# Queue order, pool opening and adding transfers in a one-core FNet and mixture-of-experts kernel

## The chip, the core and the metric

The kernel runs on one core of one Trainium2 chip. A core has a matrix engine (PE, with weight loads counted apart as PEld), three engines for element-wise work (DVE, the vector engine; ACT, the scalar engine; POOL, GpSimd) and SP, which here only issues transfers. Each engine takes its instructions from a queue of its own, in order; an instruction that waits holds up everything behind it on that engine. Transfers are issued on three queues: SP's (q1 in the profile), ACT's (q10) and POOL's (q0). The metric is the device time of one execution in microseconds (us).

## What is computed

A block of 2048 tokens with 512 features is normalised. Two things are computed from the result and added to the input: a two-dimensional Fourier mixing (two dense products with cosine and sine matrices) and a mixture of 8 experts in which every token goes to one.

```python
xn = layernorm(x)                                   # 2048 x 512
a, b = xn @ dft_hid_re.T, xn @ dft_hid_im.T         # over the features
y = dft_seq_re @ a - dft_seq_im @ b                 # over the tokens, 2048 x 2048 each
logits = xn @ w_gate                                # 512 x 8
e = first_argmax(logits)                            # one expert per token, its gate softmax over one value
out = x + y + gate * (silu(xn @ w1[e]) @ w2[e])     # w1: 512 x 1376, w2: 1376 x 512
```

## The kernel before

Every product is done with numbers split into a high and a low part (`hi` and `lo`): three matmuls, hi by hi, lo by hi and hi by lo, stand for one product. `split` (line 68) makes the parts: ACT copies `raw` to `hi`, DVE subtracts to get `lo`. `stream` (line 76) loads a 512 KB block on SP's queue into one of three `raw` slots (`RAWS`) and splits it into one of four `hi` and `lo` slots. All blocks stand in one list; `need(key, ahead)` (line 90) brings the list up to a key and some blocks further, so it sets what is written when. A transfer's issue waits until its slot is free.

In order of time, PE does this:

- **Head and first products** (to about 102 us). `two_products(0, ...)` multiplies token blocks b = 0 to 7 by the cosine blocks `c(0, 0, b)` and the sine blocks `c(0, 1, b)` of the first quarter of the outputs. Each b first needs the normalised block: `Norm` loads x, takes statistics on DVE, a root on ACT, factors on DVE, then ACT writes `xh` and `xn`, and DVE writes `xl`. The norm of b = 0 is done in two halves (`n0`, `n1`) in an order fixed by hand for DVE and ACT, together with the split of the first blocks (lines 213 to 233). The norms of later blocks are placed by `pre0(b)`. The tile framework's scheduler orders the rest on each engine, from priorities and a model of times.
- **Second quarter** (to 192 us), with the gate's logits on DVE beside it (`logits`, line 339; the gate's weights lie in `wgb`, copied to all partitions); then `count`, `route` and `scatter`, which sorts the tokens by expert into `xs` in memory.
- **`even_product(0)` and `(1)`** (to 283 us): products with sums of blocks. Their results are stored by ACT's queue to `p2`, `q6`, `v`, `c00` and `r`; `sum_up(ri)` (line 480) then adds stored blocks in memory, by three transfers on POOL's queue that add to their target.
- **Experts** (to about 579 us): 8 windows of sorted tokens, each with eleven steps `f`: `up` (weights w1), SiLU on ACT (`sil`), its split on DVE (`hh`, `hl`), and, two steps later, `down` (weights w2). Weight blocks come in the list as `w(i, k, b)`: window, matrix, block. Every fifth block of the list takes its slots from an extra pool, `more` (line 100), once that is open. It is opened at line 764, right after `head.close()`, whose place in memory it takes: its first transfer must wait until the head's last tile is released.
- **`odd_product(0)` and `(1)`** (to 648 us) and **`second_product(0 to 3)`** (to the end), with `fetch_product` loading the stored intermediate products (`pd` and others) for the last product.

At several places a line asks for its written order, `tc.keep_in_program_order`; SP's transfers have no such order in general.

Of the kernel before, what the change touches and what calls it, by code (L numbers as in the profile page):

```python
# [44 lines left out]
def fnet_moe(ctx, tc, x, cr, ci, dr, di, wg, w1, w1r, w2, w2r, out):  # L45
# [141 lines left out]
    for i in range(WARM):  # L187
# [7 lines left out]

    n0, n1 = Norm(0, 0, 1), Norm(0, 1, 1)
    first = [tuple(st.tile([P, 1024], F32 if n == "raw" else F32R, tag=n, name=n, bufs=RAWS if n == "raw" else 4)
                   for n in ("raw", "hi", "lo")) for ri in range(2)]
    halves = [slice(j * TC, (j + 1) * TC) for j in range(2)]
    for j, n in enumerate((n0, n1)):  # L200
        n.load()
        for ri in range(2):
            SY.dma_start(first[ri][0][:, halves[j]], (cr, ci)[ri][0, 0, :, j, :])

    def first_hi(ri, j):
        raw, hi, _ = (t[:, halves[j]] for t in first[ri])
        A.copy(hi, raw)

    def first_lo(ri, j):
        raw, hi, lo = (t[:, halves[j]] for t in first[ri])  # L210
        V.tensor_sub(lo, raw, hi.bitcast(F32))
# [22 lines left out]
    for ri in range(2):  # L234
        ready["c", 0, ri, 0] = first[ri][1:]
    norms = {}

    def load_x(b):
        norms[b] = Norm(b)
        norms[b].load()  # L240
# [9 lines left out]

    load_x(1)
    need(("c", 0, 1, 0), 2)
    load_x(2)
    load_x(3)
# [20 lines left out]
    wgb = ep.tile([P, E, D], F32, name="wgb", bufs=1)  # L275
# [10 lines left out]
    xtab = cst.tile([P, 3, NX], I32, name="xtab")  # L286
    regs = cst.tile([P, 2 * E], I32, name="regs")
# [59 lines left out]
    def pre0(b):  # L347
        if b + 1 < NB:
            norm(b + 1)
        if b + 4 < NB:  # L350
            load_x(b + 4)
        if 1 <= b < 3:
            g = slice(4 * (b - 1), 4 * b)
            need(("c", 0, 0, b), 2)
            SY.dma_start(wgb[:, g, :], wg[None, g, :].to_broadcast([P, 4, D]))
# [6 lines left out]
    for t, base, n in ((xs, S, 3 * P), (hr, WCUM[E], 1)):  # L362
        for r in range(0, n, P):
            m = min(P, n - r)
            A.dma_start(t[base + r:base + r + m, :], zero[:m, :])
# [18 lines left out]
    def even_parts(b):  # L384
# [5 lines left out]
        A.dma_start(xd[b], xn[b].rearrange("p j d -> p (j d)"))  # L390

    def odd_parts(b):
        r = tp.tile([P, 2, D], F32, name="other")
        tc.keep_in_program_order(SY.dma_start(r, xd[b].rearrange("p (j d) -> p j d", j=2)))
# [85 lines left out]
    def sum_up(ri):  # L480
        for a, b in (("c00", "p2"), ("r", "q6"), ("v", "r")):
            G.dma_start(out=ps[a][ri], in_=ps[b][ri], accum_op=OP.add, max_dma_last_dim=1024)
# [281 lines left out]
    more.append(mo.enter_context(tc.tile_pool(name="more", bufs=1)))  # L764

    todo = []
    for i, w in enumerate(wins):
        for f in range(NF):
# [6 lines left out]
            if f == 9 and i in (1, 2):  # L775
                sum_up(i - 1)
# [93 lines left out]


# [88 lines left out]
```

## Time and profile before

| what | value |
|---|---|
| runs of the kernel before | 737.63, 742.56 and 744.33 us, median 742.56 |
| the profiled execution's own time | 742.19 us |
| its span, first to last instruction | 740.5 us |
| PE busy | 720.4 us, 97% |
| DVE, ACT, POOL busy | 539.0, 315.6, 43.6 us |
| mean granted PE clock | 0.990 |
| moved by transfers | 163.62 MB, mean 221 GB/s |

A row of a timeline gives the start and the duration of an instruction, its engine and line, the tiles it writes and reads, how often it stands there in a row, and in brackets how long its engine had been idle before it and what ended that. The view of waits sums such idle time by the pair of lines: total, how often, the longest. The chain of waits follows back from an instruction to what released it. In a row of windows each engine has its busy time and its count; then come the granted PE clock, the busy share of the transfer engines, and GB/s.

### The profile page before, as it was taken

What the parts mean: (1) busy time and instruction counts of PE and PEld (TensorE: products, weight loads), DVE (VectorE), ACT (ScalarE), POOL (GpSimd) and SP (SyncE); (2) the same over time, 40 slices, a digit from 0 to 9 for tenths busy, and PEclk for the clock granted to TensorE, in tenths of its full rate; (3) what the DMA queues carried; (4) which work ended last, traced back from release to release, by engine and by line L of the source; (5) the groups of instructions that cost most, each with busy time, mean ns of one, the idle gap of its engine ahead of it and who ended that gap; (6) DMA issues with size and microseconds to landing.
All of it is one profiled execution on the core that took longest, in us unless ns stands there. A gap on an engine that the chain in (4) does not pass through costs nothing.

```text
span 740.5 us, 10987 instructions
## 1 busy us (share of the span) xinstructions
PE 720.4 (97%) x3940; PEld 625.3 (84%) x3940; DVE 539.0 (73%) x1073; ACT 315.6 (43%) x462; POOL 43.6 (6%) x67
## 2 busy tenths in 40 slices
PE   9899999999999999599999999999999999999997
PEld 7688888878888878599999999998999787788886
DVE  6999999859688754367777777766777787635752
ACT  4654241322444445345545555554554455412110
POOL 1000000007100101000000000000000000052100
PEclk9999999999999999799999999999999999999999
DMA  9964253367667957847565757665565679799632
GB/s 322 369 232 159 97 199 110 119 227 269 242 222 258 285 149 259 205 154 260 176 226 203 255 192 249 215 211 191 204 223 193 207 253 309 255 351 359 227 129 74
DMA packets 53864, 163.62 MB, mean 221 GB/s; under 512 B 5902, under 2 KB 10254, under 8 KB 53549
## 3 DMA queue, kind: packets, MB, share of 16 engines
q1 hardware_dynamic: 39376, 125.19, 49.1%
q10 hardware_dynamic: 8701, 26.15, 9.1%
q0 software_dynamic: 5728, 11.54, 6.0%
q8 instruction: 32, 0.52, 0.3%
q14 instruction: 27, 0.22, 0.1%
HBM read 132.38 MB, written 33.62 MB: 224 GB/s over the span
## 4 chain that ended last, share of the span: by engine, by line
PE 84%; DMA 9%; DVE 3%; ACT 2%; issue 1%; SPq 0%; ACTq 0%; DVEq 0%
PE acc L300 23%; PE up L694 6%; PE up L696 6%; PE up L695 6%; PE s L461 4%; PE s L462 4%; PE s L460 4%; PE o L858 4%; PE o L856 4%; PE o L857 4%; PE y L724 4%; PE y L725 4%; PE y L726 4%; PE y L719 2%; PE y L717 2%; PE y L718 2%
## 5 line engine op out<-in xcount | busy, mean ns | idle before, releaser
L74 DVE TENSOR_TENSOR lo<-raw,hi 128x1024 fp32r<-128x1024 f32 (+2 forms) x126 | 143.8, 1145 | 69.8 <-ACT hi L73 68.1
L73 ACT CAST hi<-raw 128x1024 fp32r<-128x1024 f32 (+2 forms) x126 | 124.6, 989 | 163.2 <-PE acc L300 79.4
L694 PE MATMUL up<-wth,hi 128*128 128x256 f32 (+10 forms) x352 | 106.1, 301 | 0.0
L300 PE MATMUL acc<-hi,xh 128*128 128x512 f32 x256 | 101.9, 400 | 3.7 <-ACT xh L175 3.7
L696 PE MATMUL up<-wth,lo 128*128 128x256 f32 (+10 forms) x352 | 102.4, 291 | 0.0
L695 PE MATMUL up<-wtl,hi 128*128 128x256 f32 (+10 forms) x352 | 102.3, 291 | 0.0
L300 PE MATMUL acc<-lo,xh 128*128 128x512 f32 x256 | 101.6, 399 | 0.0
L300 PE MATMUL acc<-hi,xl 128*128 128x512 f32 x256 | 99.0, 395 | 0.0
L461 PE MATMUL s<-lo,xh 128*128 128x512 f32 x224 | 88.6, 395 | 1.0 <-DVE lo L415 1.0
L460 PE MATMUL s<-hi,xh 128*128 128x512 f32 x224 | 88.6, 396 | 0.8 <-ACT hi L411 0.8
L462 PE MATMUL s<-hi,xl 128*128 128x512 f32 x224 | 88.2, 395 | 0.0
L343 DVE SCALAR_TENSOR_TENSOR junk<-xn,wgb 128x512 f32<-128x512 f32 x128 | 81.1, 683 | 0.0
L724 PE MATMUL y<-hh,hi 128*128 128x318 f32 (+9 forms) x220 | 65.8, 300 | 9.0 <-DVE hh L701 9.0
L695 PEld LDWEIGHTS up<-wtl,hi 128*128 128x128 f32 (+1 forms) x352 | 66.0, 187 | 0.8
L694 PEld LDWEIGHTS up<-wth,hi 128*128 128x128 f32 (+1 forms) x352 | 65.9, 187 | 0.9
L725 PE MATMUL y<-hl,hi 128*128 128x318 f32 (+9 forms) x220 | 66.0, 300 | 0.2 <-DVE hl L702 0.2
L696 PEld LDWEIGHTS up<-wth,lo 128*128 128x128 f32 (+1 forms) x352 | 65.7, 187 | 0.0
L726 PE MATMUL y<-hh,lo 128*128 128x318 f32 (+9 forms) x220 | 65.6, 298 | 0.0
L300 PEld LDWEIGHTS acc<-hi,xh 128*128 128x128 f32 x256 | 48.5, 190 | 16.0 <-ACT xh L175 4.2
L300 PEld LDWEIGHTS acc<-lo,xh 128*128 128x128 f32 x256 | 48.6, 190 | 11.8
L300 PEld LDWEIGHTS acc<-hi,xl 128*128 128x128 f32 x256 | 48.0, 187 | 11.8
L415 DVE TENSOR_TENSOR lo<-sums,hi 128x1024 fp32r<-128x1024 f32 x32 | 39.1, 1223 | 20.9 <-ACT hi L411 19.2
(198 smaller groups left out, 1228.4 us busy)
## 6 DMA issues: line engine op xcount, KB each, us to landing
raw<-in_w SPq DMA_DIRECT2D x80, 512.0 KB
raw<-in_cr SPq DMA_DIRECT2D x31, 512.0 KB
raw<-in_ci SPq DMA_DIRECT2D x31, 512.0 KB
xd<-xn ACTq DMA_DIRECT2D x8, 512.0 KB
pd<-sp ACTq DMA_DIRECT2D x8, 512.0 KB
other<-in_cr SPq DMA_DIRECT2D x8, 512.0 KB
xw<-xs SPq DMA_DIRECT2D x8, 512.0 KB
other<-in_ci SPq DMA_DIRECT2D x8, 512.0 KB
```

The costliest lines, as they stand in the source:

```text
L73: A.copy(hi, raw)
L74: V.tensor_sub(lo, raw, hi.bitcast(F32))
L300: T.matmul(acc[k], x_[b][:, j, k * P:(k + 1) * P], c_, start=(s == 0 and x_ is xh and c_ is ch), stop=(s == NT - 1 and x_ is xl))
L460: T.matmul(acc[p][k], a, ch, start=(b == 0), stop=False)
L461: T.matmul(acc[p][k], a, cl, start=False, stop=False)
L462: T.matmul(acc[p][k], al, ch, start=False, stop=(b == NB - 1))
L694: T.matmul(t[:m, :w], hi[:, c:c + m], self.xh[:, k, :w], start=(k == 0), stop=False)
L695: T.matmul(t[:m, :w], hi[:, c:c + m], self.xl[:, k, :w], start=False, stop=False)
L696: T.matmul(t[:m, :w], lo[:, c:c + m], self.xh[:, k, :w], start=False, stop=(k == KD - 1))
L724: T.matmul(y, hi[:m, c:c + P], hh[:m, :w], start=first, stop=False)
L725: T.matmul(y, hi[:m, c:c + P], hl[:m, :w], start=False, stop=False)
L726: T.matmul(y, lo[:m, c:c + P], hh[:m, :w], start=False, stop=last)
```

## The change

1. **SP's queue**: everything on SP's queue stands in the order in which the program writes it (`sp_order`), up to the closing part; before, the scheduler chose.
2. **First blocks**: the raw data of `c(0,0,0)` and `c(0,1,0)` go into `wgb`, where the gate's weights are loaded later, and no longer into two of the three `raw` slots.
3. **Head**: the norms of blocks 1 and 2, and the two blocks of b = 1, stand in the fixed order on DVE and ACT; x is loaded up to three blocks ahead of its product instead of four.
4. **Zero stores and `xd` stores**: ACT's transfers that write zeros to `xs` and `hr`, and those that store `xn` to `xd` for the odd product, keep their program order on ACT. The zero stores then stand behind the first products' stores (about 103 us in the time of before, where they were issued from 8.93 us on), the `xd` stores beside `even_parts`.
5. **`more`** is opened in window 0 at step f = 8, and not ahead of window 0. The list is unchanged, so the block that takes the first place in the extra pool is a later one.
6. **`sum_up`**: POOL first copies one column of window i + 1's transposed tokens to `mark`, and the three adding transfers are issued behind that. `sum_up(0)` goes from the time of `even_product(1)` to window 1, `sum_up(1)` from the start of window 0 to window 2.
7. **`odd_parts`**: its load no longer asks for its place by itself, since the whole queue now has the written order.

```diff
     A.activation(warm, eps, AF.Sqrt)
+    sp_order = ctx.enter_context(ExitStack())
+    sp_order.enter_context(tc.manual_schedule(engines={SY.engine}))
+
+
+    wgb = ep.tile([P, E, D], F32, name="wgb", bufs=1)
     n0, n1 = Norm(0, 0, 1), Norm(0, 1, 1)
-    first = [tuple(st.tile([P, 1024], F32 if n == "raw" else F32R, tag=n, name=n, bufs=RAWS if n == "raw" else 4)
-                   for n in ("raw", "hi", "lo")) for ri in range(2)]
+    norms = {}
+
+    def load_x(b):
+        norms[b] = Norm(b)
+        norms[b].load()
+
+    first = [(wgb[:, 2 * ri:2 * ri + 2, :], *(st.tile([P, 1024], F32R, tag=n, name=n) for n in ("hi", "lo")))
+             for ri in range(2)]
+    for ri in range(2):
+        ready["c", 0, ri, 0] = first[ri][1:]
     halves = [slice(j * TC, (j + 1) * TC) for j in range(2)]
     for j, n in enumerate((n0, n1)):
         n.load()
         for ri in range(2):
-            SY.dma_start(first[ri][0][:, halves[j]], (cr, ci)[ri][0, 0, :, j, :])
+            SY.dma_start(first[ri][0][:, j, :], (cr, ci)[ri][0, 0, :, j, :])
     def first_hi(ri, j):
-        raw, hi, _ = (t[:, halves[j]] for t in first[ri])
-        A.copy(hi, raw)
+        A.copy(first[ri][1][:, halves[j]], first[ri][0][:, j, :])
     def first_lo(ri, j):
-        raw, hi, lo = (t[:, halves[j]] for t in first[ri])
-        V.tensor_sub(lo, raw, hi.bitcast(F32))
+        V.tensor_sub(first[ri][2][:, halves[j]], first[ri][0][:, j, :], first[ri][1][:, halves[j]].bitcast(F32))
     with tc.high_priority(), tc.manual_schedule(engines={V.engine, A.engine}):
         n0.stats()
...
         first_lo(0, 1)
         n1.low()
         first_lo(1, 1)
-    for ri in range(2):
-        ready["c", 0, ri, 0] = first[ri][1:]
-    norms = {}
-
-    def load_x(b):
-        norms[b] = Norm(b)
-        norms[b].load()
+        load_x(1)
+        n = norms[1]
+        n.stats()
+        n.root()
+        n.factors()
+        n.values(xh)
+        need(("c", 0, 0, 1), 0)
+        n.values(xn)
+        n.low()
+        need(("c", 0, 1, 1), 0)
+        load_x(2)
+        n = norms[2]
+        n.stats()
+        n.root()
+        n.factors()
+        n.values(xh)
+        n.values(xn)
+        n.low()
     def norm(b):
         n = norms[b]
...
         n.values(xn)
         n.low()
-    load_x(1)
-    need(("c", 0, 1, 0), 2)
-    load_x(2)
-    load_x(3)
-
     ident = cst.tile([P, P], F32, name="ident")
     make_identity(nc, ident)
...
     up1 = ramp("up1", 1, 0)
     down1 = ramp("down1", -1, E)
     upx = ramp("upx", 1, 0, NX)
-    wgb = ep.tile([P, E, D], F32, name="wgb", bufs=1)
     junk = ep.tile([P, 2, D], F32, name="junk", bufs=1)
     wsz, wcm = cst.tile([P, E], F32, name="wsz"), cst.tile([P, E], F32, name="wcm")
     for i in range(E):
...
     posx = cst.tile([P, NT], I32, name="posx")
     gate = cst.tile([P, NT], F32, name="gate")
     xtab = cst.tile([P, 3, NX], I32, name="xtab")
+    mark = cst.tile([P, 2], F32, name="mark")
     regs = cst.tile([P, 2 * E], I32, name="regs")
...
             n -= 1
     def pre0(b):
-        if b + 1 < NB:
+        if 2 < b + 1 < NB:
             norm(b + 1)
-        if b + 4 < NB:
-            load_x(b + 4)
+        if b + 3 < NB:
+            load_x(b + 3)
         if 1 <= b < 3:
             g = slice(4 * (b - 1), 4 * b)
             need(("c", 0, 0, b), 2)
...
     for t, base, n in ((xs, S, 3 * P), (hr, WCUM[E], 1)):
         for r in range(0, n, P):
             m = min(P, n - r)
-            A.dma_start(t[base + r:base + r + m, :], zero[:m, :])
+            tc.keep_in_program_order(A.dma_start(t[base + r:base + r + m, :], zero[:m, :]))
...
         tc.keep_in_program_order(V.tensor_sub(t, x_(0, 1), x_(0, 0)))
         V.tensor_sub(t, t, x_(1, 1))
         parts(b, slice(DH, 2 * DH), t)
-        A.dma_start(xd[b], xn[b].rearrange("p j d -> p (j d)"))
+        tc.keep_in_program_order(A.dma_start(xd[b], xn[b].rearrange("p j d -> p (j d)")))
     def odd_parts(b):
         r = tp.tile([P, 2, D], F32, name="other")
-        tc.keep_in_program_order(SY.dma_start(r, xd[b].rearrange("p (j d) -> p j d", j=2)))
+        SY.dma_start(r, xd[b].rearrange("p (j d) -> p j d", j=2))
         x_ = quarters(r)
         t = tp.tile([P, 2 * TC], F32, name="sums")
         tc.keep_in_program_order(V.tensor_sub(t[:, :DH], x_(0, 0), x_(0, 1)))
...
         for a, to in zip(acc, (("c00", "r"), ("p2",), ("q6",), ("v",))):
             out_of(a, xp, 4, *(ps[n][ri] for n in to))
-    def sum_up(ri):
-        for a, b in (("c00", "p2"), ("r", "q6"), ("v", "r")):
-            G.dma_start(out=ps[a][ri], in_=ps[b][ri], accum_op=OP.add, max_dma_last_dim=1024)
+    def sum_up(ri, after):
+
+        with tc.issue_after(G.tensor_copy(mark[:, ri:ri + 1], after).ins):
+            for a, b in (("c00", "p2"), ("r", "q6"), ("v", "r")):
+                G.dma_start(out=ps[a][ri], in_=ps[b][ri], accum_op=OP.add, max_dma_last_dim=1024)
     def odd_product(ri, mid=None):
         acc = []
...
     even_product(1, lambda b: wins[0].turn(b - NB + KD) if b >= NB - KD else None)
     need(("w", 0, 0, 0), 2)
     head.close()
-    more.append(mo.enter_context(tc.tile_pool(name="more", bufs=1)))
     todo = []
     for i, w in enumerate(wins):
...
             if 0 < i < 5 and f in (3, 8):
                 odd_parts(2 * (i - 1) + f // 8)
             if f == 9 and i in (1, 2):
-                sum_up(i - 1)
+                sum_up(i - 1, wins[i + 1].xl[:, 0, :1].bitcast(F32))
+            if i == 0 and f == 8:
+                more.append(mo.enter_context(tc.tile_pool(name="more", bufs=1)))
             if i + 1 < E:
                 if f == 1:
                     wins[i + 1].load()
...
     for c in range(NCH):
         second_product(c, rest(c), c + 1 if c + 1 < NCH else None)
     tail.close()
+
+    sp_order.close()
     xsize = nc.values_load(xtab[0:1, 2, 0:1], min_val=0, max_val=NX,
```

On ACT, at the start of the experts, the casts and SiLUs stood so. Here `hi_2656`, `hi_2734` and `hi_2662` are the high parts of three weight blocks, of which the second, from `raw_2732`, is in the extra pool (w(0,0,3), for `up` steps 6 and 7), and `raw_2660` is w(0,1,2), for `down` steps 4 and 5; the `sil` are those of steps 0 to 4.

```order
L698 ACT_TABLE_LOAD
L698 ACTIVATE sil_2626<-up_2613 128x318
L698 ACTIVATE sil_2645<-up_2632 128x318
L73 CAST hi_2656<-raw_2654 128x1024
L698 ACTIVATE sil_2679<-up_2666 128x318
L73 CAST hi_2734<-raw_2732 128x1024
L73 CAST hi_2662<-raw_2660 128x1024
L698 ACTIVATE sil_2714<-up_2701 128x318
L73 CAST hi_2740<-raw_2738 128x1024
L698 ACTIVATE sil_2757<-up_2744 128x318
```

In the changed kernel the same place reads as follows; `raw_2658` is w(0,1,2) and `raw_2730` w(0,0,3), now both in the ordinary slots.

```order
L717 ACT_TABLE_LOAD
L717 ACTIVATE sil_2624<-up_2611 128x318
L717 ACTIVATE sil_2643<-up_2630 128x318
L73 CAST hi_2654<-raw_2652 128x1024
L717 ACTIVATE sil_2677<-up_2664 128x318
L73 CAST hi_2660<-raw_2658 128x1024
L717 ACTIVATE sil_2712<-up_2699 128x318
L73 CAST hi_2732<-raw_2730 128x1024
L717 ACTIVATE sil_2755<-up_2742 128x318
L73 CAST hi_2738<-raw_2736 128x1024
```

The cast of w(0,0,3) has moved from before the SiLU of step 3 to behind it, and w(0,1,2)'s now stands before that SiLU.

On DVE, in the head, the end of the first blocks' split and the norm of block 1 stood so; `raw_236` and `raw_242` are the cosine and the sine block of b = 1, and the chain `r0_230`, `t0_231`, `r1_232`, `mr_233` holds the factors of block 1's norm (x_255 and x_264 belong to blocks 2 and 3).

```order
L74 TENSOR_TENSOR lo_239<-raw_236,hi_238 128x1024
L164 RECIPROCAL r0_230<-sd_228 128x2
L156 BN_AGGR mv_248<-bn_392 128x2
L155 BN_STATS bn_395<-x_255 128x6
L166 TENSOR_TENSOR t0_231<-r0_230 128x2
L155 BN_STATS bn_480<-x_264 128x6
L74 TENSOR_TENSOR lo_245<-raw_242,hi_244 128x1024
L167 TENSOR_TENSOR t0_231<-t0_231,vh_229 128x2
L156 BN_AGGR mv_248<-bn_395 128x2
L156 BN_AGGR mv_257<-bn_480 128x2
L168 SCALAR_TENSOR_TENSOR r1_232<-t0_231,r0_230 128x2
```

In the changed kernel `raw_251` and `raw_260` are the two blocks of b = 1.

```order
L164 RECIPROCAL r0_230<-sd_228 128x2
L166 TENSOR_TENSOR t0_231<-r0_230 128x2
L167 TENSOR_TENSOR t0_231<-t0_231,vh_229 128x2
L168 SCALAR_TENSOR_TENSOR r1_232<-t0_231,r0_230 128x2
L169 SCALAR_TENSOR_TENSOR mr_233<-mv_227,r1_232 128x2
L74 TENSOR_TENSOR lo_254<-raw_251,hi_253 128x1024
L181 TENSOR_TENSOR xl1_99<-xn1_113,xh1_91 128x1024
L74 TENSOR_TENSOR lo_263<-raw_260,hi_262 128x1024
```

The subtractions of b = 1's two blocks have moved behind the factors of its norm.

On SP, in the head, the loads behind the first blocks stood so (`raw` from `in_cr` and `in_ci` are cosine and sine blocks, `x` the token blocks):

```order
L150 DMA x_234<-in_x 128x2x512
L78 DMA raw_236<-in_cr 128x1024
L150 DMA x_255<-in_x 128x2x512
L150 DMA x_264<-in_x 128x2x512
L78 DMA raw_242<-in_ci 128x1024
L150 DMA x_342<-in_x 128x2x512
L78 DMA raw_419<-in_cr 128x1024
```

and now so:

```order
L150 DMA x_234<-in_x 128x2x512
L78 DMA raw_251<-in_cr 128x1024
L78 DMA raw_260<-in_ci 128x1024
L150 DMA x_273<-in_x 128x2x512
L150 DMA x_352<-in_x 128x2x512
L150 DMA x_409<-in_x 128x2x512
L78 DMA raw_411<-in_cr 128x1024
```

The sine block of b = 1 has moved ahead of the loads of token blocks 2 and 3.

## The prediction

> **What bounds the kernel now.** The page comes first: PE is busy for nearly the whole span (the third row is ACT's queue: packets, MB, share of 16 transfer engines).
>
> ```profile
> span 740.5 us, 10987 instructions
> PE 720.4 (97%) x3940; PEld 625.3 (84%) x3940; DVE 539.0 (73%) x1073; ACT 315.6 (43%) x462; POOL 43.6 (6%) x67
> q10 hardware_dynamic: 8701, 26.15, 9.1%
> ```
>
> No matmul is removed, so the change can only win what PE loses by standing still or by running slowly. The second view is PE's waits over the whole run (total, how often, longest):
>
> ```profile
> PE y L724 <- DVE hh L701: 9.0, 2, 7.8
> PE acc L300 <- ACT xh L175: 3.7, 1, 3.7
> PE spare L188 <- DVE eps L191: 1.1, 1, 1.1
> PE s L461 <- DVE lo L415: 1.0, 1, 1.0
> PE s L460 <- ACT hi L411: 0.8, 1, 0.8
> ```
>
> They lie at three places: the head, the start of the experts, the end of the odd product (the `s` rows). The third view is windows behind the two long waits; before the last two columns stands the granted clock, (x) counts matmuls:
>
> ```profile
> 23.14:26.55 3.41, 3.41 (x9) 2.65 (x8) 3.38 (x10) 3.41 (x6) 0.00 (x0) 0.50 0.94 342
> 26.56:29.97 3.41, 3.41 (x16) 2.74 (x15) 3.41 (x8) 1.79 (x4) 0.00 (x0) 1.00 1.07 305
> 303.04:313.28 10.24, 4.53 (x16) 4.30 (x17) 6.88 (x10) 4.87 (x7) 1.01 (x1) 0.50 0.72 196
> ```
>
> Behind each long wait PE runs at half clock. In the head 9 matmuls stand where the next window has 16: 7 × 3.41 / 16 = 1.5 us lost. At the experts the half clock covers 16 matmuls behind the wait; the chain below has them at 0.27 us, and 0.15 once the clock is full: 16 × 0.12 = 1.9 us. So there are 3.7 + 1.5 = 5.2 us to be had in the head, 7.8 + 1.9 = 9.7 at the experts, 1.8 at the odd product's end.
>
> **Experts: parts 5 and 6.** The chain of waits around this place:
>
> ```profile
> 286.59 9.48 DMA v<-sp
> 296.28 8.57 DMA raw<-in_w
> 307.17 1.22 DVE lo L74
> 308.75 0.64 PE y L724
> 312.29 0.27 PE y L726
> 313.52 0.15 PE up L695
> ```
>
> and ACT's timeline, with one row of DVE's:
>
> ```profile
> 287.54 1.23 DVE L74 TENSOR_TENSOR lo<-raw,hi 128x1024 fp32r<-128x1024 f32 x1 [3.40 <-ACT hi L73]
> 291.65 1.05 ACT L73 CAST hi<-raw 128x1024 fp32r<-128x1024 f32 x1 [2.07 <-DMA raw<-in_w]
> 304.95 1.99 ACT L73 CAST hi<-raw 128x1024 fp32r<-128x1024 f32 x2 [11.92 <-DMA raw<-in_w]
> 306.85 0.43 ACT L698 ACTIVATE sil<-up 128x318 f32<-128x318 f32 x1
> ```
>
> The SiLU at 306.85 is step 3's; PE waits for its `hh`. It is late only because ACT stands, in order, before the cast of w(0,0,3), whose raw data go to the `more` slot. That load could not leave before the head's last store, `v<-sp`, had landed (9.48 us), and then took 8.57.
>
> Now w(0,0,3) takes an ordinary slot, free when w(0,1,1) has been subtracted (287.54 + 1.23): it leaves at 288.8, 7.5 us earlier. With 8.57 us again it lands at 297.4; cast (1.05) and subtraction (1.22) end at 299.7. The stalled `down` begins at 300.9 (308.75 less the 7.8 of the waits), and w(0,0,3) is wanted one `down` later, so it has 1 us and that step's 12 matmuls of 0.15, 3 us in all. Step 3's SiLU now stands behind the cast of w(0,1,2), whose load follows directly behind the one that ended the wait at 291.65. It lands up to 8.57 us later; I take 3, at 294.6. Cast, SiLU and `hh` (1.05 + 0.43 + 0.36, the last from 308.39, where the subtraction ends, to 308.75) end at 296.5, where 300.9 is wanted; at 8.57 us they end 1.2 late. What is late next: the `more` block waits for the head's release too, but the pool's first block is now one of window 1, asked for when that release is 10 us past. I take the whole 9.7 us. The low end is 6: a load 3 us later than that, and some of the half clock.
>
> Part 6 takes the adding transfers out of this stretch and puts them into windows 1 and 2, near 360 and 400 us. Their price shows from 296.3 to 300.3 us, where three weight loads lay on SP's queue (q1) beside them (q0):
>
> ```profile
> q0 software_dynamic: 578, 0.58, 107.1%
> q1 hardware_dynamic: 1, 0.00, 0.3%
> ```
>
> SP's queue moved nothing in 4 us. The Trainium skill, page "DMA: Bandwidth & Descriptors", section "Queues, rings and completion order", says that each transfer engine serves its queues in turn, a packet at a time; by that, a weight load beside an adding transfer would only be slowed and the starving rival below would fall away. The trace does not show such turns here, so that rival keeps its chance.
>
> I take a standstill: one adding transfer kept the next waiting 9.23 us (first row below), so loads may be held for about 10.
>
> ```profile
> 259.37 1.00 POOL L482 DMA_DIRECT2D v<-r  x1 [9.23 <-DMA r<-q]
> ACT hi L73 <- PE up L695: 15.7, 14, 2.7
> 240.00:260.00 20.00, 20.00 (x87) 16.07 (x86) 15.83 (x18) 9.40 (x11) 2.84 (x3) 1.00 1.01 292
> ```
>
> The second row leads ACT's waits from 330 to 440 us: casts wait for PE to free a `hi` slot, and no load stands among these waits, so blocks lie ready ahead of their casts. A late cast reaches PE only after more slack: at the experts ACT stood 11.92 us, PE 7.8. From 240 to 260, with all three transfers of `sum_up(0)` in it, PE did not pause. Cost: zero; at worst a wait of 3 us in each window (10 less some 4 of that slack and as much of the blocks lying ready, rounded up).
>
> **Head: parts 1 to 3.** SP, ACT, DVE and PE in the timelines:
>
> ```profile
> 7.98 0.69 DVE L155 BATCH_NORM_STATS2 bn<-x 128x6 f32<-128x512 f32 x1
> 11.20 0.12 DVE L169 SCALAR_TENSOR_TENSOR mr<-mv,r 128x1 f32<-128x1 f32 x1
> 11.96 0.34 SPq L78 DMA_DIRECT2D raw<-in_ci  x1
> 13.52 0.68 DVE L211 TENSOR_TENSOR lo<-raw,hi 128x512 fp32r<-128x512 f32 x1
> 17.04 1.05 ACT L73 CAST hi<-raw 128x1024 fp32r<-128x1024 f32 x1 [2.50 <-DMA raw<-in_ci]
> 18.12 1.22 DVE L74 TENSOR_TENSOR lo<-raw,hi 128x1024 fp32r<-128x1024 f32 x1 [1.12 <-ACT hi L73]
> 20.23 0.14 DVE L169 SCALAR_TENSOR_TENSOR mr<-mv,r 128x2 f32<-128x2 f32 x1
> 21.27 1.52 ACT L175 ACTIVATE xh<-x,mr,r 128x512 fp32r<-128x512 f32 x2
> 22.14 0.50 PE L300 MATMUL acc<-hi,xh 128*128 128x512 f32 x1 [3.75 <-ACT xh L175]
> ```
>
> The sine block of b = 1 found no `raw` slot until 11.96; its cast and subtraction stood ahead of block 1's last factors on DVE (18.12, 20.23). Now its load has a slot from the start, and the factors stand first. The first blocks' last subtraction ends at about 13.0 (before 14.2, with two `bn_stats` of 0.69 ahead of it that now follow). Block 1's statistics and factors take 3.2 us, as from 7.98 to 11.20, where one statistic of its own and two of another block stood: `mr` at 16.1. Two `xh` (1.52) end at 17.6, the cast at 18.7; PE is free at 18.39 (22.14 - 3.75). Subtraction and `xl` (1.22 each) end at 19.9 and 21.3, where PE, four matmuls of 0.23 (20 us / 87) between, wants them at 19.6 and 20.8. So 0.3 + 0.3 + 0.5 us remain.
>
> Block 1's 48 matmuls last 11.0 us; PE then wants `xh` of b = 2 at 18.4 + 1.1 + 11.0 = 30.5. On DVE its factors stand behind the sine subtraction of b = 1 (to 22.5), two subtractions of b = 2, four statistics, one logit (0.69, a statistic's width) and about eight small ones of 0.14: 22.5 + 2.4 + 2.8 + 0.7 + 1.1 = 29.5; two `xh` end at 31.0, 0.5 late. `xl` of b = 2 stands behind five logits and a subtraction: 29.5 + 3.5 + 1.2 + 1.2 = 35.4, where PE, 16 matmuls on, wants it at 34.7. In all 0.3 + 0.3 + 0.5 + 0.5 + 0.7 = 2.3, in pieces far below 3.7, so without half clock. Gain 5.2 - 2.3 = 2.9; ends 0 (DVE's order as late as the old one) and 4.8. It is not eaten up behind: from b = 3 to 192 us no wait stands in PE's table.
>
> **Odd product's end: parts 1 and 7.** The chain:
>
> ```profile
> 635.51 6.98 DMA raw<-pd
> 643.59 1.22 DVE pl L74
> 644.81 1.15 DVE lo L415
> ```
>
> The scheduler put fetches for much later products between those for the next one on SP's queue; a `pd` fetch of 0.5 MB took 6.98 us, and its subtraction stood ahead of the `lo` that PE wanted. In written order only what is needed first is fetched there: 1.7 back, ends 0 and 1.8. In turn the `pd` for the second of the tail's products leaves some 8 us later, into the tail's fullest stretch (next to last column: transfer engines' share):
>
> ```profile
> 660.00:680.00 20.00, 20.00 (x90) 16.56 (x89) 12.92 (x16) 2.71 (x4) 9.12 (x9) 1.00 1.00 377
> 174.00:212.00 38.00, 38.00 (x164) 30.54 (x163) 29.70 (x48) 15.74 (x23) 10.93 (x10) 1.00 0.74 259
> ```
>
> A product of the tail lasts some 20 us, two to three fetches of 6.98; I take 0, at worst 3.
>
> **Part 4.** The `xd` stores are 8 × 0.5 MB; at ACT's queue's rate (9.1% of 740.5 us for 26.15 MB, 2.6 us per MB) that is 10 us of all transfer engines, inside 174 to 212: 38 us that are 0.74 full become 1.0 full. Loads will come later there; PE waited for none, so I take 0, at worst 2. The zero stores are small, and what they feed is read after 283 us: 0.
>
> **Rivals.**
> - *Adding transfers starve windows 1 and 2.* If they hold the weights beyond the slack, each `sum_up` repeats before's stall and half clock, once for its first two transfers and once for `v<-r`; three of the four times make 3 × 9.7 = 29 us, 728.5 + 29 = 757, slower. For it: q1's row. Against: 240 to 260, and that no cast waits for a load there. It decides from a load about 10 us late. The mild form, 3 us in each window, gives 734.
> - *The head's wait only moves* to b = 2, with the half clock: 728.5 + 2.9 = 731.
> - *The written order blocks SP*: one issue that waits for a slot holds all loads behind it, in the odd product, the tail or beside the `xd` stores: 3 to 7 us, 731 to 735. PE's short list of waits says that the loads have room today; nothing shows how much.
> - *The experts' wait stays in part* (w(0,0,3) or w(0,1,2) late): 3 to 9 us, 731 to 737.
> - *The change doesn't do what it says*: for ACT and DVE the rows of the order exclude it.
>
> **How the numbers follow.** The profiled execution took 742.19 us, 0.4 below the median of the runs. 742.2 - 9.7 - 2.9 - 1.7 = 727.9, against the median 728.3; call it 728.5. With all of 5.2 + 9.7 + 1.8 gone it is 725.9, about the floor. Chances: forecast, 725 to 731: 0.55; head only moved 0.12; SP's order or part 4 0.12; experts in part 0.09; mild waits in the windows 0.07; starved 0.05. About 1% is what a measurement of this kernel can tell from no change: below 735.1 is faster. Faster: 0.55 + 0.12 + 0.10 + 0.05 + 0.05 = 0.87, less 0.05 for stretches not costed: 0.82. Slower: the starved case and 0.01 of that, 0.06; the rest, 0.12, is the same. The range from 725 to 735 leaves out the starved case, the tops of three others, and what was not costed: 0.05 + 0.08 + 0.05.
>
> **What would show it.** Right: no `hh` wait beyond 1.2 us near 300, the clock full there, the load of w(0,0,3) leaving near 289; two `xh` of b = 1 ending near 17.6 and full clock behind; no 7 us `pd` fetch before the odd product's last `lo`. Wrong: a weight load among ACT's or PE's waits in windows 1 and 2, half clock anywhere behind the warm-up, or a wait of PE for `xl` or `xh` of b = 2 above 2 us.

## The result and the profile after

The changed kernel took 721.83 us in the median of four runs (721.72 to 725.22); the kernel before, in four runs beside it, 742.09 (737.63 to 744.33). The ratio is 0.9745, with a 95% interval from 0.9692 to 0.9799: faster, and by 3 us more than the low end of the predicted range (725). The profiled execution took 721.72 us, its span is 719.8 us. The page and PE's waits:

```profile
span 719.8 us, 10962 instructions
PE 710.7 (99%) x3940; PEld 622.6 (86%) x3940; DVE 537.5 (75%) x1073; ACT 316.1 (44%) x462; POOL 44.5 (6%) x69
...
PE y L743 <- DVE hh L720: 1.2, 1, 1.2
PE spare L188 <- DVE eps L191: 1.1, 1, 1.1
PE s L478 <- DVE lo L432: 0.2, 1, 0.2
PE y L744 <- DVE hl L721: 0.2, 1, 0.2
```

All three places are almost empty: gone are the head's 3.7 us, the experts' 7.8 and 1.5 of the odd product's 1.7 (0.75 and 0.96 us; the rounded rows make it 1.8). What stays are two waits that the kernel before has too (1.2 and 1.1) and small ones. The window that had 9 matmuls at half clock in the head now has 17 at full clock:

```profile
23.14:26.55 3.41, 3.41 (x17) 2.79 (x16) 3.41 (x9) 1.24 (x2) 0.00 (x0) 1.00 1.08 393
```

That is not the whole gain. The span fell by 740.45 - 719.85 = 20.6 us. PE's idle time before its last matmul fell from 15.8 to 2.8, 13.0 us; the two half-clock stretches gave 1.5 + 1.9 = 3.4. Of the 4.2 left over, the windows below show where it came from. They are 60 us of the first products, without any wait, in the kernel before and then in the changed one:

```profile
40.00:100.00 60.00, 60.00 (x259) 48.21 (x258) 59.09 (x169) 24.14 (x32) 0.00 (x0) 1.00 0.44 160
```

```profile
40.00:100.00 60.00, 60.00 (x264) 49.23 (x263) 60.00 (x176) 27.81 (x38) 0.00 (x0) 1.00 0.37 125
```

PE is busy all the time and at full clock in both, with the same matmuls, and yet five more of them fit. Taken over all matmuls of the first, the even and the odd products (lines 300 and 460 to 462 of the kernel before), the starts lie 233.3 ns apart before and 229.0 after. 1440 of them make 1440 × 4.3 ns = 6.2 us. On the other side the stretch from PE's last matmul to the end grew from 4.25 to 6.33 us, 2.1. The sum is 13.0 + 3.4 + 6.2 - 2.1 = 20.5; the 3.4 is the prediction's estimate, the other three are read from the two traces.

### The profile page after: what moved, and what is told of

Its sections match the earlier page's. It is cut to its first block, busy times and chain, and to the rows that moved or that the text cites. A ratio compares the mean times of both kernels' runs of the same rounds, so it can differ in the third digit from the quotient of the medians.

```text
span 719.8 us, 10962 instructions
## 1 busy us (share of the span) xinstructions
PE 710.7 (99%) x3940; PEld 622.6 (86%) x3940; DVE 537.5 (75%) x1073; ACT 316.1 (44%) x462; POOL 44.5 (6%) x69
## 4 chain that ended last, share of the span: by engine, by line
PE 88%; DVE 5%; DMA 4%; ACT 2%; issue 1%; ACTq 0%; DVEq 0%
PE acc L317 23%; PE up L713 6%; PE up L714 6%; PE up L715 6%; PE s L479 5%; PE s L478 5%; PE s L477 5%; PE y L744 4%; PE y L745 4%; PE o L878 4%; PE o L876 4%; PE y L743 4%; PE o L877 4%; PE y L736 2%; PE y L737 2%; PE y L738 2%
## 5 line engine op out<-in xcount | busy, mean ns | idle before, releaser
L317 PE MATMUL acc<-hi,xh 128*128 128x512 f32 x256 | 99.7, 394 | 0.0
L317 PE MATMUL acc<-lo,xh 128*128 128x512 f32 x256 | 99.6, 393 | 0.1
L876 PE MATMUL o<-dh,ph 128*128 128x512 f32 (+1 forms) x136 | 51.2, 377 | 0.0
```

Source lines behind the costliest of these rows:

```text
L317: T.matmul(acc[k], x_[b][:, j, k * P:(k + 1) * P], c_, start=(s == 0 and x_ is xh and c_ is ch), stop=(s == NT - 1 and x_ is xl))
```

## Experiments: the pace of the products

The change moved tiles about in the on-chip memory without meaning to. In these products `xh` and `xl` are the stationary side of a matmul, 128 x 128 weights that PE loads for each one, and `hi` and `lo` the streamed side, 512 columns. `mark`, the new tile of 8 bytes, takes 32 bytes, and everything allocated behind it on the left side begins 32 bytes later; and since the first blocks no longer take `raw` slots, the `hi` and `lo` slots now lie ahead of the `raw` slots (whole multiples of 512 bytes, so this does not change their place modulo 512). The stationary tiles `xh` and `xl`, on the right side, stayed. The built programs give the addresses: modulo 512, `hi` and `lo` began at 256 before and at 288 now, `xh` and `xl` at 480 in both.

The changed kernel was run four times, beside the kernel before at 742.09 us; the runs below stand beside the kernel before at 740.4 to 741.3. Differences from the changed kernel's 721.83 us are to be read with that in mind.

**Two kernels before, with unused bytes.** The edit, with 8 or 24 numbers of 4 bytes:

```diff
     regs = cst.tile([P, 2 * E], I32, name="regs")
+    cst.tile([P, 8], F32, name="pad")
```

> The kernel before with one unused 32-byte tile, so that every tile allocated behind it on the left (the blocks' hi, lo and raw, the expert tiles) begins 32 bytes later; nothing else differs. Theory A (the pace of the product matmuls depends on where the streamed tile lies against the stationary one: before, hi and lo began 32 bytes off xh and xl modulo 64, in the changed kernel at the same place modulo 64): matmuls of the two products go from 233.4 to about 229 ns, 1440 of them, 6 us less, 736 us, with all waits as before. Theory B (the faster pace came from the other order of work or of transfers): 233 ns, no change, 742 us.

> The kernel before with 96 unused bytes; hi and lo then lie at the same place as xh and xl modulo 128. Theory A in its wider form (the place modulo 128 counts, as in the tail's matmuls, where both sides lie alike modulo 128 and take 226.7 ns): 226.7 ns, 1440 x 6.7 = 9.6 us less, 732.5 us. Theory A modulo 64 alone: 229 ns, 736 us. Theory B: 742 us.

With 32 bytes: 736.32 us against 740.52, ratio 0.9922 (0.9896 to 0.9949), and the changed kernel's pace, without any of its order:

```profile
40.00:100.00 60.00, 60.00 (x264) 49.24 (x263) 59.80 (x170) 25.06 (x34) 0.00 (x0) 1.00 0.45 161
```

The starts lie 229.0 ns apart, and theory B falls. The gain is 4.2 us and not 6; in the profile the waits came out differently too (6.2 us at the experts, and 2.9 at the odd product, with a half-clock window behind). With 96 bytes: 739.31 us, ratio 0.9984 (0.9961 to 1.0008), 232.4 ns. Both forms of A fall too: modulo 128 it should have been 226.7, modulo 64 229 ns.

**Two changed kernels with unused bytes**, by the same edit with 8 and 16 numbers.

> The changed kernel with 32 unused bytes: hi and lo lie 32 bytes off xh and xl modulo 64 again, as before the change. Theory A: 233 ns, 6 us more than the changed kernel, 728 us, which is what the prediction had. Theory B: 229 ns, 722 us.

> The changed kernel with 64 unused bytes: hi and lo at the same place as xh and xl modulo 128. Theory A modulo 128: 226.7 ns, 1440 x 2.3 = 3.3 us less than the changed kernel, 718.5 us, better than both. Theory A modulo 64 alone, and theory B: 722 us.

They took 727.43 and 726.24 us, at 233.4 and 232.4 ns. 32 bytes more bring back the old pace and 5.6 us. With that pace the changed kernel takes what the prediction's sum gave (727.9), which is the first half of the answer to where it went wrong. The second run missed all its expectations (718.5 and 722 us), so neither modulo 128 nor modulo 64 is the rule.

**The difference modulo 512.** With the rule open, one run moved both kinds of tiles to the same place modulo 512 (48 unused numbers), and one moved only the stationary ones:

```diff
     xl = [per.tile([P, 2, D], F32R, name=f"xl{b}") for b in range(NB)]
+    per.tile([P, 8], F32, name="pad")
```

> The changed kernel with 192 unused bytes: hi and lo then lie at the same place as xh and xl modulo 512 (480), as the two sides of the tail's matmuls do. Theory A1 (the difference of the two places modulo 512 sets the pace; zero is the best, 226.7 ns as in the tail): 719.0 us or so, 3 us less than the changed kernel. Theory A2 (the place of the streamed tile alone, modulo 128, and 32 is the best of the four): it lies at 96, 232.4 ns as with 64 unused bytes, 726 us.

> The changed kernel with 32 unused bytes on the right, so that only xh and xl (the stationary sides) move, by -32 bytes; hi and lo stay. Theory A1 (the difference counts): it is now 160 modulo 512, as with 32 unused bytes on the left: 233.4 ns, 728 us. Theory A2 (the streamed tile's place alone): 229 ns, 722 us.

Both came as theory A1 said. With the same place on both sides (first window) the kernel took 719.3 us, ratio 0.9706 (0.9686 to 0.9727), faster than the kernel before and the changed one; with `xh` and `xl` moved, `hi` and `lo` where they were (second window), it took 727.8 us.

```profile
40.00:100.00 60.00, 60.00 (x267) 49.67 (x266) 60.00 (x174) 27.79 (x38) 0.00 (x0) 1.00 0.38 130
```

```profile
40.00:100.00 60.00, 60.00 (x258) 48.26 (x258) 59.61 (x172) 27.89 (x38) 0.00 (x0) 1.00 0.36 122
```

The last of this group does the alignment alone, in the kernel before (56 unused numbers).

> The kernel before with 224 unused bytes: hi and lo at the same place as xh and xl modulo 512, nothing else changed. Theory A1 (the difference of the two places modulo 512 sets the pace): product matmuls at 227 instead of 233.4 ns, 1440 x 6.4 = 9.2 us less, all waits as before: 731 to 733 us. Rival (the gain from this place needs the changed order): 736 us or more.

It took 733.97 us, ratio 0.9911 (0.9878 to 0.9944), at 226.9 ns: 7.1 us less, a little less than expected, with the long waits all still there (4.0 in the head, with two half-clock windows instead of one, and 7.4 at the experts). The nine kernels with a stated place, by the bytes from `hi` up to `xh` modulo 512:

| difference | kernels | ns from start to start |
|---|---|---|
| 224 | before | 233.3 |
| 192 | changed; before + 32 | 229.0; 229.0 |
| 160 | changed + 32; changed with `xh` at -32 | 233.4; 233.4 |
| 128 | before + 96; changed + 64 | 232.4; 232.4 |
| 0 | before + 224; changed + 192 | 226.9; 227.0 |

In these nine, kernels of different order agree wherever the difference agrees, and the tail's matmuls, whose two sides differ by 0, take about 227 ns in all. Differences between those of the table, and why it is so, were not tried; the `raw` slots kept the same place modulo 512 as `hi` and `lo` in all nine, so a part of theirs is not excluded.

The place is not all, though. In two kernels further down (part 6 undone; parts 2 and 3 undone) the mean pace at 192 was 230.6, and it is a mixture: 229.0 ns up to 150 or 151 us, 233.3 from there to the end of the even products, 229.0 again behind the experts, with no tile moved. The step comes at the two small matmuls of `count`; they stand at 151 us in the changed kernel too, without such a step. At 192 two paces are thus possible; what decides between them is open.

## Experiments: the start of the experts

**Part 5 undone**: the extra pool opens ahead of window 0 again, the adding transfers stay held back.

```diff
     head.close()
+    more.append(mo.enter_context(tc.tile_pool(name="more", bufs=1)))
...
-            if i == 0 and f == 8:
-                more.append(mo.enter_context(tc.tile_pool(name="more", bufs=1)))
```

> The changed kernel with part 5 undone: the extra pool opens ahead of window 0 again, the adding transfers stay held back. The prediction's account: w(0,0,3) again waits for the last store v<-sp of the even product (296 in before's time) and its cast stands before the SiLU of step 3, but its load no longer competes with adding transfers and takes about 4 us instead of 8.6; PE waits some 3 us for hh, perhaps with a half clock of 1 to 2 us: 725 to 727 us. Rival (the adding transfers alone made the wait): no wait, 722 us. Second rival (the store also lands late): the whole 9.7 us, 731 us.

726.61 us, 4.8 more than the changed kernel. From this kernel, the chain at the place, and PE's wait:

```profile
277.09 9.32 DMA v<-sp
...
286.63 3.17 DMA raw<-in_w
...
293.35 0.25 DVE hh L720
```

```profile
PE y L743 <- DVE hh L720: 3.4, 2, 2.2
```

The store holds the load for 9.3 us as before (9.5), but the load then takes 3.17 us where it took 8.57; of PE's 7.8 us, 2.2 come back, with one window of half clock. The first account is right. With the early pool, holding the adding transfers thus seems to help (2.2 us of wait where 7.8 stood, though parts 1 to 4 differ too); part 6 alone in the kernel before was not run.

**Part 6 undone**: the adding transfers start as soon as their stores are done.

```diff
-        with tc.issue_after(G.tensor_copy(mark[:, ri:ri + 1], after).ins):
-            for a, b in (("c00", "p2"), ("r", "q6"), ("v", "r")):
-                G.dma_start(out=ps[a][ri], in_=ps[b][ri], accum_op=OP.add, max_dma_last_dim=1024)
+        for a, b in (("c00", "p2"), ("r", "q6"), ("v", "r")):
+            G.dma_start(out=ps[a][ri], in_=ps[b][ri], accum_op=OP.add, max_dma_last_dim=1024)
```

> The changed kernel with part 6 undone: the adding transfers start as soon as their stores are done, sum_up(1) at the start of window 0 and sum_up(0) during the second even product; the extra pool opens late. The prediction's account: w(0,0,3) leaves about 7 us earlier than in the kernel before and is mostly in before the first adding transfer; the next load, w(0,1,3), stands still for 5 to 9 us, which its slack of about one down and one up step does not fully cover: 722 to 725 us. Rival (the adding transfers alone made the wait): 6 to 10 us, 728 to 732 us.

722.51 us. PE waits at the experts only for the first SiLU's table, 1.2 us as everywhere:

```profile
PE y L742 <- DVE hh L719: 1.2, 1, 1.2
PE spare L188 <- DVE eps L191: 1.1, 1, 1.1
```

So holding the adding transfers is worth nothing there once the pool opens late. (This kernel is one of the two at 230.6 ns; 527 matmuls at 233.3 in place of 229.0 ns cost its profiled execution 2.2 us.) That is confirmed from the other side.

**Part 5 alone**, in the kernel before, by the same edit turned round.

> The kernel before with part 5 alone: the extra pool opens at step 8 of window 0; adding transfers, head, stores and SP's order as before, tiles as before. Theory (part 5 alone takes away the experts' wait, since undoing part 6 in the changed kernel brought none back): 7.8 and 1.9 us less, 731 to 732 us. Rival (parts 5 and 6 are both needed there): a wait of 2 to 6 us stays, 734 to 740 us.

730.33 us against 741.08, ratio 0.9854 (0.9805 to 0.9902): 10.8 us by the medians, and no wait for `hh` beyond the first SiLU's, while the head's wait stays.

```profile
PE acc L300 <- ACT xh L175: 3.4, 1, 3.4
PE y L724 <- DVE hh L701: 1.2, 1, 1.2
```

**The adding transfers in their new place** need no run of their own; the changed kernel shows them. From 384 to 388 us, in window 2, the queues and, from 320 to 440, one of ACT's waits:

```profile
q0 software_dynamic: 545, 0.53, 84.0%
q1 hardware_dynamic: 136, 0.49, 32.9%
```

```profile
ACT hi L73 <- DMA raw<-in_w: 7.8, 6, 3.0
```

Weight loads go on beside the adding transfers, but these 4 us are an average of two things. Where both queues have work, here from 381.5 to 385 us, they move packets in nearly equal numbers (of 4 KB on q1, of 1 KB on q0):

```profile
q1 hardware_dynamic: 231, 0.88, 67.0%
q0 software_dynamic: 241, 0.24, 42.2%
```

From 385.82 to 387.54 us SP's queue moved nothing: new loads, issued from 385.57 on, were slow to start. In the kernel before this was longer: its three loads were issued from 296.28 to 297.47 us, when SP's queue had been idle since 293.7, and the first packet moved at 300.18, 3.9 us after the first issue. With part 5 undone, where no adding transfer runs, the load issued at 286.63 us began at 287.59, after 1.0 us. So the prediction's 4 us without a packet were the late start of new loads, and not queued loads held back. ACT waited for loads six times, 3.0 us at most, and PE never. The change thus brought the wait for loads that the prediction named as a sign of its being wrong, and its slack covered it.

## Experiments: head, stores and SP's order

The head of the changed kernel first, from the timelines of DVE and ACT: block 1's factors, the cast of b = 1's cosine block, then block 2's factors and `xl`:

```profile
15.74 0.16 DVE L169 SCALAR_TENSOR_TENSOR mr<-mv,r 128x2 f32<-128x2 f32 x1
17.36 1.04 ACT L73 CAST hi<-raw 128x1024 fp32r<-128x1024 f32 x1
28.22 0.14 DVE L169 SCALAR_TENSOR_TENSOR mr<-mv,r 128x2 f32<-128x2 f32 x1
32.14 1.22 DVE L181 TENSOR_TENSOR xl<-xn,xh 128x1024 fp32r<-128x1024 f32 x1
```

Predicted were 16.1, then a cast ending at 18.7 (18.4 measured), 29.5, and `xl` ending at 35.4 (33.4). Each step came 0.2 to 2 us sooner than counted, and PE waited 0.07 us in place of 2.3. Four runs undid one part each.

**SP's order** (parts 1 and 7): `sp_order` and its close removed, `odd_parts` asks for its place again.

> The changed kernel with parts 1 and 7 undone: the scheduler again sets the order on SP's queue (all tiles stay where they are). The prediction's account: the fetches for later products come in between again and the 1.7 us at the odd product's end return, the rest stays: 723 to 724 us. Rival (the written order is also what brings the head's loads in time): another 2 to 5 us in the head, 726 to 729 us. Rival (the order does nothing): 722 us.

725.2 us (721.88 to 727.57), between the first two expectations. PE's waits in its profile:

```profile
PE acc L315 <- ACT xh L175: 1.2, 1, 1.2
...
PE s L476 <- DVE lo L430: 0.9, 1, 0.9
PE acc L315 <- ACT hi L73: 0.9, 1, 0.9
PE s L475 <- ACT hi L426: 0.7, 1, 0.7
```

The odd product's waits return (1.7 us in these rows), and 2.5 in the head in pieces too short to lower the clock. Its end, though, takes 4.26 us again and not 6.3: the written order costs 2.1 us there.

**The fixed order of the norms** (part 3): blocks 1 and 2 go back to `norm(b + 1)` in `pre0` (the diff shows this line alone) and the lines of their fixed order are gone; loads stay as written. **The raw slots** (part 2): `first` takes its raw data from the slots again, behind `hi` and `lo`, so that no product tile moves.

```diff
-        if 2 < b + 1 < NB:
+        if b + 1 < NB:
             norm(b + 1)
```

```diff
-    first = [(wgb[:, 2 * ri:2 * ri + 2, :], *(st.tile([P, 1024], F32R, tag=n, name=n) for n in ("hi", "lo")))
-             for ri in range(2)]
+    first = [tuple(st.tile([P, 1024], F32R, tag=n, name=n) for n in ("hi", "lo")) for ri in range(2)]
+    first = [(st.tile([P, 1024], F32, tag="raw", name="raw", bufs=RAWS).rearrange("p (j t) -> p j t", j=2), *f) for f in first]
```

> The changed kernel with part 3 undone: the scheduler places the norms of blocks 1 and 2 and the split of the blocks of b = 1; the first blocks' raw data stay in the gate's place, SP in written order. Theory (the order on DVE made the head's wait): some of it returns, 2 to 5 us with the half clock, 724 to 727 us. Rival (the missing raw slot alone made it): 722 us.

> The changed kernel with part 2 undone: the first blocks' raw data take two of the three raw slots, so the sine block of b = 1 leaves at about 12 us and lands near 17 again; the order on DVE and ACT stays fixed. Theory (the order on DVE made the head's wait): PE wants that block only 24 matmuls, 5.5 us, behind the cosine block, so 722 to 723 us. Rival (the missing slot alone made it): 3.7 and 1.5 us return, 727 us.

722.15 and 721.69 us, neither to be told from the changed kernel, and no head wait in either beyond 0.2 us. Each could have covered for the other, so both were undone together.

> The changed kernel with parts 2 and 3 both undone (the first blocks in raw slots, the norms of blocks 1 and 2 placed by the scheduler); tiles of the products stay where they are. Theory (either of the two suffices, so each undone alone cost nothing): the head's wait of 3.7 us and the half clock of 1.5 come back, 726 to 727 us. Rival (the written order on SP or the held stores took the wait away): 722 us.

721.36 us, no head wait: the rival. Neither part 2 nor part 3 is needed. The sine block of b = 1 leaves late (12.14 us) and its subtraction comes late here too, but it no longer matters, since the scheduler itself now puts block 1's factors ahead of it:

```profile
12.88 0.16 DVE L169 SCALAR_TENSOR_TENSOR mr<-mv,r 128x2 f32<-128x2 f32 x1
...
17.06 1.22 DVE L74 TENSOR_TENSOR lo<-raw,hi 128x1024 fp32r<-128x1024 f32 x1 [1.14 <-ACT hi L73]
```

**The held stores** (part 4): both `keep_in_program_order` removed.

```diff
-            tc.keep_in_program_order(A.dma_start(t[base + r:base + r + m, :], zero[:m, :]))
+            A.dma_start(t[base + r:base + r + m, :], zero[:m, :])
...
-        tc.keep_in_program_order(A.dma_start(xd[b], xn[b].rearrange("p j d -> p (j d)")))
+        A.dma_start(xd[b], xn[b].rearrange("p j d -> p (j d)"))
```

> The changed kernel with part 4 undone: the scheduler places the zero stores and the stores of xn. The prediction's account: nothing waited for them and nothing waits now: 721 to 723 us. Rival (in the head they take transfer time from the first loads): 1 to 3 us more, 723 to 725 us.

726.67 us, 4.8 more; both expectations were too low. PE's wait and the chain to it:

```profile
PE acc L317 <- ACT xh L175: 2.4, 1, 2.4
```

```profile
22.30 6.88 DMA raw<-in_cr
...
29.25 1.06 ACT hi L73
...
30.33 1.23 DVE lo L74
...
31.86 0.82 ACT xh L175
```

The zero stores (from 8.89 us on) and the stores of `xn` (11.96 and 20.74 us) are back among the head's loads; a cosine block of b = 3 takes 6.88 us, and its subtraction stands on DVE ahead of block 2's factors. It is the mechanism of the old wait, one block later, and one window of half clock follows. So the part that was priced at nothing carries the head; which of the two kinds of stores does it was not tried. Part 4 was then done alone, in the kernel before.

> The kernel before with part 4 alone (zero stores and the stores of xn in program order); SP's order, the raw slots and the norms are the scheduler's as before, tiles as before. In its order on DVE the factors of block 1 now stand ahead of the subtraction of the sine block of b = 1, though no line of the norms is changed. Theory (the stores in ACT's queue are what pushed the factors back in the scheduler's order, and their absence also frees the head's transfers): the head's wait of 3.7 us and its half clock of 1.5 go, 736 to 737 us. Rival (the late sine block itself makes the wait): 741 us.

733.7 us against 741.33, ratio 0.9899 (0.9865 to 0.9933), 2.3 us below what the theory gave. In its head:

```profile
12.69 0.16 DVE L169 SCALAR_TENSOR_TENSOR mr<-mv,r 128x2 f32<-128x2 f32 x1
...
17.63 1.21 DVE L74 TENSOR_TENSOR lo<-raw,hi 128x1024 fp32r<-128x1024 f32 x1
```

```profile
PE y L724 <- DVE hh L701: 7.8, 2, 6.5
PE spare L188 <- DVE eps L191: 1.1, 1, 1.1
PE acc L300 <- ACT xh L175: 0.2, 1, 0.2
PE y L725 <- DVE hl L702: 0.2, 1, 0.2
```

Block 1's factors are done at 12.7 us where they were done at 20.2, and the head's wait is gone, by a change that names no line of the norms: it changed what the scheduler made of DVE's order. Freed transfers alone would not explain it: the subtraction that stood ahead of the factors comes only 0.5 us sooner (17.63 for 18.12). Why the stores move DVE's order is not shown. The odd product's waits are gone in this profile as well; why is not shown. They come and go among kernels that share that stage's order on SP: the kernel before with 224 unused bytes has none at the very end and 1.2 us earlier.

The last run kept parts 4 to 6 and undid all the others of the head and SP.

> The changed kernel with parts 1, 2, 3 and 7 undone together; parts 4, 5 and 6 stay, and the tiles of the products stay where they are. Theory (the held stores, part 4, keep the factors ahead of the subtraction on DVE, so the head's long wait stays away; SP's order costs what it did when undone alone): 723 to 726 us. Rival (the three parts of the head are together what took the wait away): 728 to 730 us.

722.43 us (720.05 to 724.64), and a profiled span of 718.2, below that of the changed kernel. Parts 1, 2, 3 and 7 together are worth nothing that these runs can tell.

## Experiment: the end

The written order lengthens the end by some 2 us in all its kernels (6.2 to 6.4 us with it, 4.2 to 4.4 without). The run closes it ahead of the tail's last product, together with the 192 unused bytes:

```diff
     for c in range(NCH):
+        if c == NCH - 1:
+            sp_order.close()
         second_product(c, rest(c), c + 1 if c + 1 < NCH else None)
...
-    sp_order.close()
```

> The changed kernel with 192 unused bytes, as tried above (719.3 us), and SP's written order closed ahead of the tail's last product. Theory (the written order lengthens the stretch from PE's last matmul to the end by 2.1 us, 6.2 to 6.4 us in every run with it and 4.2 to 4.3 without, through how SP's last stretch stands): 717.2 us with 4.2 us at the end. Rival (it comes from SP's order or program further ahead): 719.3 us, 6.2 at the end.

719.05 us, and 6.27 us behind the last matmul: the rival. It comes from something further ahead in SP's program. The traces show SP waiting 2.8 us between its last branch and its first semaphore, where the kernel before waits 0.4; from 716 us on no data moves on any queue. What it waits for stays open. This kernel and the one with 192 bytes alone are the fastest measured (ratios 0.9704 and 0.9706 to the kernel before).

## Why the prediction was wrong, and where it was right

- **"No matmul is removed, so the change can only win what PE loses by standing still or by running slowly", and the floor of 725.9**: this step failed. PE's pace at full clock was taken as fixed. Moving the tiles by 32 bytes was worth 6.2 us of pace, and that is the size of the miss: the sum without it, 727.9, stands beside the 727.4 us of the changed kernel at the old pace (the head's 2.3 us too little and the end's 2.1 us, below, cancel). The row that could have warned is in the prediction itself: 0.23 us for 512 columns in the products, where the tail's 660 to 680 window has 90 matmuls in 20 us against 87 from 240 to 260.
- **Experts, 9.7 us**: right in size (7.8 - 0 and the half clock), and right that part 5 takes it. The step-3 cast came in time, as counted. **Part 6, cost zero**: right; but the standstill that its rival rested on was misread: the 4 us were the late start of new loads. Once loads run, they and the adding transfers share the transfer engines (231 and 241 packets in the rows above), which is what the rule of the Trainium skill says (page "DMA: Bandwidth & Descriptors", section "Queues, rings and completion order"). Why a load starts 3.9 us late beside adding transfers is not shown. The stretch from 240 to 260 us, too, held only two of the three adding transfers: the third was issued at 259.37. What part 6 gains was not told apart from part 5 in the prediction: nothing once the pool opens late, by two runs.
- **Head, 2.9 us**: mis-sized, 5.2 came. The remaining 2.3 us were a sum of estimates for DVE's order, all too late (with a slip: 19.9 and 1.22 make 21.1, not 21.3). And the cause was put in the wrong part: the late factors were the wait, as said, but the raw slots and the fixed order are not needed to move them. "The zero stores are small ... 0" and "I take 0" for the `xd` stores is the second step that failed: held alone, they took 7.6 us from the kernel before. In its profile 3.6 us of the head's wait and the half clock there are gone, and also the odd product's 1.7 and 1.3 us of the experts'.
- **Odd product's end, 1.7 us**: 1.5 came. That nothing else would be fetched there was wrong as a reason: in the changed kernel a `pd` fetch still takes 6.3 us, and the subtraction behind it still stands ahead of a `lo` that PE wants; only the wait is now 0.2 us.

```profile
601.02 6.32 DMA raw<-pd
```

- **The tail**: its loads, leaving later, cost nothing, as taken. The 2.1 us at the very end were in no term.
- **The starving rival, 757 us**: did not come; ACT waited 3.0 us at most for a load.

## What to carry to other kernels

Before pricing a change, ask whether it moves tiles: a new tile of a few bytes or a pool opened in another order shifts all that lies behind it, and a pace per matmul, read from two windows without waits, shows it at once. When a scheduler sets the order, undo the parts one at a time and also do them alone: here two parts out of seven, the late pool and the held stores, and an accident of addresses seem to make the whole gain (alone they took 10.8, 7.6 and 4.2 us from the kernel before, 22.6 against 20.3; the three were not run together without the rest), and the part that looked most like a head repair was not needed.

## What the runs showed of the hardware that was not expected

The pace of float matmuls of 512 columns with 128 x 128 weights follows how the two operands' places in the on-chip memory differ modulo 512 bytes: 226.9 ns at 0, 229.0 at 192, 232.4 at 128, 233.4 at 160, 233.3 at 224, the same in two or more kernels at each (at 224 the kernels before with part 4 or part 5 alone). In the kernel before it is 233.3 ns both from 40 to 100 us, where the transfer engines are 0.44 busy, and from 240 to 260, where the share is 1.01. At 192 a second pace, 233.3 ns, held from 151 us to the end of the even products in two profiles.

A weight load issued onto an idle queue beside adding transfers moved its first packet after 3.9 us, and after 1.0 us without them; loads under way shared the engines with them in nearly equal numbers of packets.

A window of half clock, 3.41 us long, followed single waits of PE of 3.75, 2.4 and 2.2 us, and once (the kernel before with 32 unused bytes, from 640.6 us) two waits of 0.9 us that lay 1.5 us apart; two such waits in the kernel before, of 0.75 and 0.96 us, brought none.
